# A fused attention and gated-convolution kernel on one Trainium2 core: k's last pieces ahead of the second q piece, half of w_in as two loads, and a new order on all engines

## The chip, the cores and the metric

The kernel runs on one core of a Trainium2 chip. The metric is device microseconds of one launch, as the median of several runs. A core has five engines that each work through their own instructions in order and wait for each other by semaphores: TensorE (PE; its weight loads are PEld), VectorE (DVE), ScalarE (ACT), GpSimd (POOL) and SyncE (SP). Matmuls write to PSUM, of which this kernel uses eight banks. Transfers are issued by POOL (loads that convert fp32 to bf16), by SP (loads, stores, transposes) and by ACT; they share 16 DMA engines. In the profile q0 is POOL's queue of transfers and q1 is SP's.

## What is computed

An attention without softmax, a norm over each head, then a feed-forward layer with a gate from a convolution of three taps over the sequence.

```python
def _attn_ref(q, k, v, g_norm):                  # (8, 8, 576, 64) each
    kv = np.einsum('bhsd,bhse->bhde', k, v)
    out = np.einsum('bhsd,bhde->bhse', q, kv)
    rms = np.sqrt(np.mean(out * out, axis=-1, keepdims=True) + 1e-06)
    return (out / rms * g_norm)
...
def _moe_ref(x, w_in, conv_w, w_out):            # x: (8, 576, 512), d_ff 1024
    h = np.maximum(x @ w_in, 0.0)
    ...
    for k in range(K):                           # K = 3, over the sequence
        conv_out += conv_w[k][None, None, :] * hp[:, k:k + S, :]
    gate = 1.0 / (1.0 + np.exp(-conv_out))
    return (h * gate @ w_out)
```

Inputs and output are fp32; the kernel computes in bf16 with fp32 sums.

## The kernel before

**Tiling.** There are eight batches, each with eight heads in four pairs. A pair of heads fills the 128 partitions (two times 64), with the 576 positions of the sequence as 64 partitions by 9 groups of 64 columns. A load of a whole batch of q, k or v is thus a tile of 128 x 4 x 576. Pairs are handled in two units `u` of two pairs, and the sequence in two halves `s`. Batch 0 is loaded as fp32 in pieces by SP and ACT (`HEAD` in `pre`) and cast on chip; batch 1 comes in two loads for each of q, k and v, and batches 2 to 7 in one each, from POOL.

**Steps.** For a batch: `kv` makes k transposed times v, and `kva` or `kvd` copies it out of PSUM on ACT or DVE; `qt` transposes q on TensorE and `qa` or `qd` copies it; `ot` multiplies the two; `sq`, `on` or `oq`, `nl` and `mo` do the norm and leave `x`. Then `hk`, `hs` or `hm` multiply `x` by a block `f` of 128 columns of w_in, and `rp`, `rh` or `re` apply the relu on ACT into `h`; `ta`, `aa`, `ab` (DVE), `sg` (ACT) and `mg` (DVE) make the gate and apply it; `om` multiplies 128 rows `m` of a pair of batches `p` by w_out in two halves of four blocks, `ea` (ACT) or `ed` (DVE) copies the 128 x 512 result into a buffer of the ring `row`, and `st` stores it from SP. The last rows are done in two halves of 256 columns (`oh`, `eh`, `dh`, `sh`).

**Batches 6 and 7** differ: q is transposed by a DMA (`tq`, two for each batch, one for each unit, issued on SP), k times v is done by `kz`, its result is copied to swapped partitions by two small DMAs (`kx`, SP), and `ox`, `ss`, `ln`, `sl`, `sp` and `mu` do the norm for two batches at a time.

**What sets the order.** The string `ORDER` lists every step of the kernel, with the buffer numbers behind `@`; the program is written out in that order, and a last loop ties each engine's instructions to it. A step such as `tq.6.0@1` is batch 6, unit 0, buffer 1. So each engine, and each queue of transfers, does its share of the steps in the order of the string, and a step that has to wait holds up all that stands behind it on its engine. `L` steps are loads on POOL: `Lq`, `Lk`, `Lv` with batch, first pair and number of pairs, `Li` with first block and number of blocks of w_in, `Lo` for w_out. A load writes a buffer that an earlier batch has used and so waits for that batch's last reader. `fi.n.512` is n matmuls of zeros that nothing reads.

Of the kernel before, what the change touches and what calls it, by code (L numbers as in the profile page):

```python
# [59 lines left out]
pre@0,1 af cad.q.0.0@0 cad.v.0.0@0 fi.10.512@0 qt.0.0.0@2 qd.0.0.0@0 gt.k.1.0 Li.0.4 fi.9.512@0 ct@0 Lq.1.0.2@1  # L60
Lk.1.0.2@0 Lv.1.0.2@1 Li.4.4 ps pg fi.4.512@1 cad.k.1.0@1 caa.v.1.0 caa.k.0.0 kv.0.0.1@4 kva.0.0.1@0 ot.0.0.0@6 pc
cad.v.3.0 cad.k.2.0 fi.2.512@0 cad.k.3.0 caa.q.1.0 qt.0.1.0@2 qd.0.1.0@1 sq.0.0.0@0 oq.0.0.0@4 fi.2.512@0 dg.1
caa.v.2.0 kv.0.1.1@0 fi.2.512@2 nl.0.0.0@0 kva.0.1.1 ot.0.1.0@4 sq.0.1.0@1 cad.q.0.1 qt.0.0.1@2 qa.0.0.1 fi.2.512@0
oq.0.1.0@0 nl.0.1.0@1 mo.0.0.0@0 cad.q.1.1 qt.0.1.1@6 qd.0.1.1 mo.0.1.0 ot.0.0.1@2 sq.0.0.1@2 ot.0.1.1@6 fi.1.512@0
sq.0.1.1@3 oq.0.0.1@0 nl.0.0.1@2 fi.1.512@4 fi.1.512@4 hk.0.1.0.0@4 hk.0.1.0.1 rp.1.0@0 on.0.1.1@0 nl.0.1.1@3
hk.0.2.0.0@5 hk.0.2.0.1 rp.2.0 dg.3 mo.0.0.1 dg.2 hk.0.3.0.0@4 hk.0.3.0.1 hk.0.0.0.0@2 hk.0.0.0.1 rp.0.0 hk.0.0.1.0@3
rp.3.0 hk.0.1.1.0@5 hk.0.3.1.0@0 mo.0.1.1 hk.0.3.1.1 rp.3.1 hk.0.1.1.1 rp.1.1 hk.0.0.1.1 rp.0.1 dg.0 hk.0.2.1.0@1
hk.0.2.1.1 qt.1.0.0@6 kv.1.0.1@4 rp.2.1 cv.0.2@2 sc.0.2@0 cv.0.3@0 qd.1.0.0@2 kvd.1.0.1@1 ot.1.0.1@6 sc.0.3 pl
sq.1.0.1@4 cv.0.1@4 cv.0.0@2 Lq.1.2.2 Lk.1.2.2 Lv.1.2.2 sc.0.1@1 fi.2.512@0 qt.1.1.0@0 qd.1.1.0@3 mg.0.1.1 Lo.0.8
sc.0.0 mg.0.1.0 oq.1.0.1@4 nl.1.0.1@4 mo.1.0.1@1 fi.1.512@2 hk.0.5.1.0@2 hk.0.5.0.0@3 hk.0.5.0.1 rp.5.0 hk.0.5.1.1  # L70
rp.5.1 ta.0.1.5@0 hk.0.4.1.0@0 hk.0.4.1.1 rp.4.1 hk.0.7.0.0@1 hk.0.7.0.1 kv.1.1.1@4 kvd.1.1.1 rp.7.0 ot.1.0.0@2
sq.1.0.0@5 hk.0.7.1.0@6 hk.0.7.1.1 rp.7.1 ta.0.1.7@1 ot.1.1.1@0 sq.1.1.1@6 oq.1.0.0@4 nl.1.0.0@5 mo.1.0.0 hk.0.4.0.0@6
hk.0.4.0.1 rp.4.0 hk.0.6.1.0@7 hk.0.6.1.1 rp.6.1 oq.1.1.1@4 nl.1.1.1@6 mo.1.1.1 hk.0.6.0.0@6 Lq.2.0.4@2 hk.0.6.0.1
rp.6.0 ta.0.1.4 hk.1.6.1.0@7 ta.0.1.6 hk.1.0.1.0@2 ot.1.1.0@4 sq.1.1.0@7 aa.0.1.2 hk.1.1.1.0@3 hk.1.2.1.0@6 hk.1.6.1.1
rh.1.6.1 hk.1.1.1.1 rh.1.1.1 on.1.1.0@0 nl.1.1.0@7 mo.1.1.0 hk.1.2.1.1 hk.1.5.1.0@7 hk.1.5.1.1 rh.1.5.1 rh.1.2.1
hk.1.3.1.0@3 hk.1.3.1.1 rh.1.3.1 hk.1.0.1.1 rh.1.0.1 ab.0.1.2 sg.0.1.5 sg.0.1.4 qt.2.1.0@0 qt.2.0.0@6 hk.1.5.0.0@3
hk.1.5.0.1 rh.1.5.0 qd.2.0.0@4 hk.1.0.0.0@2 hk.1.4.1.0@4 hk.1.4.1.1 hk.1.0.0.1 hk.1.1.0.0@5 hk.1.6.0.0@6 hk.1.1.0.1
hk.1.2.0.0@7 hk.1.2.0.1 rh.1.2.0 rh.1.1.0 rh.1.0.0 hk.1.6.0.1 rh.1.6.0 aa.0.1.3 qd.2.1.0@0 ab.0.1.3 sg.0.1.7 sg.0.1.6
hk.1.7.0.0@0 mg.0.1.2 hk.1.7.1.0@1 hk.1.7.1.1 rh.1.7.1 hk.1.7.0.1 rh.1.7.0 ta.1.1.1@0 ta.1.1.0 Lk.2.0.4@1 Lv.2.0.4@0
Lq.3.0.4@0 Lk.3.0.4@0 Lv.3.0.4@1 Lq.4.0.4@1 aa.1.1.0 hk.1.4.0.0@3 om.0.1.0.4@2 rh.1.4.1 hk.1.4.0.1 rh.1.4.0  # L80
om.0.2.0.4@5 kv.2.0.2@6 mg.0.1.3 om.0.1.4.4 ab.1.1.0 sg.1.1.0 sg.1.1.1 kvd.2.0.2@2 ot.2.0.1@0 sq.2.0.1@0 ed.0.1@0
st.0.1 qt.3.1.0@6 qd.3.1.0@1 Lk.4.0.4@1 Lv.4.0.4@0 Lq.5.0.4@2 om.0.2.4.4 on.2.0.1@2 qt.3.0.0@6 qd.3.0.0@2 nl.2.0.1@8
mo.2.0.1@2 om.0.3.0.4@4 ea.0.2@1 ot.2.1.1@6 ot.2.1.0@2 mg.1.1.0 om.0.3.4.4 ed.0.3@2 sq.2.1.0@1 sq.2.1.1@2 on.2.1.0@0
nl.2.1.0@9 mo.2.1.0 om.0.0.0.4@5 hk.1.3.0.0@4 on.2.1.1@0 st.0.2 nl.2.1.1@0 mo.2.1.1 om.0.0.4.4 ed.0.0@3 ot.2.0.0@2
# [54 lines left out]
def kernel(  # L139
# [46 lines left out]
    T = {}  # L186
# [638 lines left out]
```

## Time and profile before

| | us |
|---|---|
| median of 3 runs | 177.97 (177.71 to 178.49) |
| span of the profiled execution, first to last instruction | 175.6 |
| median less span | 2.4 |
| TensorE busy | 167.9 |
| VectorE busy | 149.5 |
| ScalarE busy | 148.9 |
| POOL's loads, share of the 16 DMA engines over the span | 49.2% |

The profile is of one execution, and its own time is known by its span; the 2.4 us between the span and the median stand for start and end around it. A row of the timeline gives start, duration, engine, line, operation, tiles and count, and in brackets how long the engine had been idle and what ended that. A row of the DMA view gives the transfer, the queue, the count, the size and the time from issue to landing; asked for a short window, it tells of the transfers that were issued in it. A row of a DMA queue gives packets, MB, and the time of the packets as a share of the window on 16 engines; it can pass 100% because packets overlap. The granted TensorE clock is 1.000 over the span.

### The profile page before, as it was taken

Reading aid. Unit: us, or ns where it says so; the run is one execution under the profiler, and the core shown is the slowest. Engines: PE = TensorE matmul, PEld = TensorE weight load, DVE = VectorE, ACT = ScalarE, POOL = GpSimd, SP = SyncE. Lnnn points to the kernel's source line nnn. Section 1 sums busy time; section 2 is a strip of 40 time slices with the busy share of each in tenths; the row PEclk is TensorE's granted clock in tenths of the full one; section 3 lists DMA queues with packets and bytes.
Section 4 is the critical chain, followed back from the end, with each engine's and each line's share of the span. In section 5 each row is a group of like instructions: output and inputs, shape, how many; then the busy total and the mean of one; then the engine's idle time right before and its main releaser. Section 6 shows DMA issues by size and latency. Waiting matters only on the chain.

```text
span 175.6 us, 5070 instructions
## 1 busy us (share of the span) xinstructions
PE 167.9 (96%) x2097; PEld 100.0 (57%) x2114; DVE 149.5 (85%) x290; ACT 148.9 (85%) x268; POOL 22.2 (13%) x35
## 2 busy tenths in 40 slices
PE   7979999999999999999999999999999999999992
PEld 2334766676447677644467764444877744444451
DVE  2796638899688899999999998989999999999950
ACT  2368899999978999999999998999999967676721
POOL 3094512200603013030000000000000000000000
PEclk9999999999999999999999999999999999999999
DMA  5999999999999999999999050330310003064486
GB/s 159 392 323 207 207 207 207 208 208 209 207 241 230 227 207 207 170 182 197 258 181 161 14 134 0 119 123 0 119 63 0 0 0 116 13 239 175 179 304 237
DMA packets 25911, 29.11 MB, mean 166 GB/s; under 512 B 6036, under 2 KB 20384, under 8 KB 25888
## 3 DMA queue, kind: packets, MB, share of 16 engines
q0 software_dynamic: 13296, 14.50, 49.2%
q1 hardware_dynamic: 12048, 13.11, 26.2%
q10 hardware_dynamic: 544, 1.18, 1.7%
q8 instruction: 16, 0.26, 0.6%
q14 instruction: 7, 0.06, 0.1%
HBM read 32.52 MB, written 9.44 MB: 239 GB/s over the span
## 4 chain that ended last, share of the span: by engine, by line
PE 76%; DVE 12%; ACT 5%; DMA 3%; issue 3%; ACTq 0%; DVEq 0%
PE banks L732 32%; PE banks L628 14%; PE banks L613 9%; PE banks L658 4%; DMA stg<-in_v_dram 3%; PE banks L460 3%; DVE h L722 2%; PE banks L708 2%; ACT taps L698 2%; PE banks L402 2%; PE banks L593 2%; PE banks L433 1%; PE banks L528 1%; DVE taps L681 1%; PE banks L286 1%
## 5 line engine op out<-in xcount | busy, mean ns | idle before, releaser
L732 PE MATMUL banks<-w_out_sb,h 128*128 128x512 bf16 x267 | 62.8, 379 | 1.2 <-issue 0.6
L698 ACT ACTIVATE taps<-taps,cw 128x576 bf16<-128x576 bf16 (+1 forms) x44 | 40.6, 958 | 5.7 <-DVE taps L692 5.5
L732 PEld LDWEIGHTS <-h 128*128 128x128 bf16 x280 | 26.2, 98 | 30.0 <-issue 1.1
L628 PE MATMUL banks<-x,w_in_sb 128*128 128x288 bf16 (+2 forms) x256 | 34.2, 286 | 0.0
L640 ACT ACTIVATE h<-banks 128x288 bf16<-128x288 f32 (+2 forms) x80 | 29.5, 460 | 0.3 <-PE banks L658 0.2
L628 PEld LDWEIGHTS <-w_in_sb 128*128 128x128 bf16 x256 | 24.4, 98 | 7.8 <-issue 0.8
L722 DVE TENSOR_TENSOR h<-h,taps 128x1152 bf16<-128x1152 bf16 (+1 forms) x24 | 22.8, 952 | 1.2 <-ACT taps L698 1.2
L687 DVE TENSOR_TENSOR taps<-taps 128x1152 bf16<-128x1152 bf16 (+1 forms) x22 | 21.5, 978 | 0.5
L509 ACT ACTIVATE sq<-banks 128x576 bf16<-128x576 f32 (+2 forms) x32 | 20.8, 691 | 1.1 <-PE banks L460 1.1
L692 DVE TENSOR_TENSOR taps<-taps,h 128x1152 bf16<-128x1152 bf16 (+1 forms) x22 | 21.4, 972 | 0.3
L681 DVE TENSOR_SCALAR taps<-h,cw 128x576 bf16<-128x576 bf16 (+1 forms) x44 | 18.7, 424 | 0.6 <-ACT h L665 0.5
L682 DVE TENSOR_SCALAR taps<-h,cw 128x576 bf16<-128x576 bf16 (+1 forms) x44 | 18.4, 418 | 0.0
L738 ACT ACTIVATE row<-banks 128x512 f32<-128x512 f32 x23 | 13.5, 597 | 5.7 <-PE banks L732 4.2
L658 PE MATMUL banks<-x,w_in_sb 128*128 128x288 bf16 (+2 forms) x128 | 17.7, 286 | 0.1
L613 PE MATMUL banks<-x,w_in_sb 128*128 128x288 bf16 x128 | 16.9, 286 | 0.0
L556 DVE SCALAR_TENSOR_TENSOR x<-banks,cw,rs 128x576 bf16<-128x576 f32 (+2 forms) x16 | 13.0, 816 | 3.9 <-ACT rs L545 3.6
L658 PEld LDWEIGHTS <-w_in_sb 128*128 128x128 bf16 x128 | 12.0, 98 | 4.4 <-issue 0.5
L227 ACT ACT_TABLE_LOAD x10 | 12.8, 1283 | 2.0 <-issue 1.8
L613 PEld LDWEIGHTS <-w_in_sb 128*128 128x128 bf16 x128 | 12.3, 98 | 3.7 <-issue 0.2
L443 DVE COPY qT<-banks 128x1152 bf16<-128x1152 bf16 (+2 forms) x13 | 8.8, 681 | 5.7 <-PE banks L433 5.7
L545 ACT ACTIVATE rs<-banks,eps_sb 128x576 f32<-128x576 f32 (+2 forms) x16 | 11.8, 740 | 1.1 <-PE banks L528 1.1
L599 DVE SCALAR_TENSOR_TENSOR x<-o,cw,banks 128x576 bf16<-128x576 f32 (+2 forms) x16 | 12.1, 810 | 0.7 <-PE banks L593 0.5
(89 smaller groups left out, 162.9 us busy)
## 6 DMA issues: line engine op xcount, KB each, us to landing
out_dram<-row SPq DMA_DIRECT2D x35, 256.0 KB, 2.3
q_sb<-in_q_dram POOLq DMA_DIRECT2D x6, 576.0 KB, 17.9
k_sb<-in_k_dram POOLq DMA_DIRECT2D x6, 576.0 KB, 14.5
v_sb<-in_v_dram POOLq DMA_DIRECT2D x6, 576.0 KB, 17.9
stg<-in_v_dram ACTq DMA_DIRECT2D x2, 576.0 KB, 6.2
stg<-in_k_dram SPq DMA_DIRECT2D x4, 288.0 KB, 6.9
w_in_sb<-in_moe_w_in_dram POOLq DMA_DIRECT2D x2, 512.0 KB, 9.9
w_out_sb<-in_moe_w_out_dram POOLq DMA_DIRECT2D x1, 1024.0 KB, 15.5
```

The source lines that it names most:

```text
L509: nc.scalar.activation(T["sq", b, u, s], T["o", b, u, s], AX.Square)
L613: nc.tensor.matmul(ps[:, s, :HS], w_in_sb[:, t, f * P:(f + 1) * P], T["x", b][:, t, c0:c1], start=(t == 0), stop=(t == NT - 1))
L628: nc.tensor.matmul(ps, w_in_sb[:, t, f * P:(f + 1) * P], T["x", b][:, t, c0:c1], start=(t == 0), stop=(t == NT - 1))
L640: nc.scalar.activation(h, fr, AX.Relu)
L658: nc.tensor.matmul(T[at], w_in_sb[:, t, f * P:(f + 1) * P], T["x", b][:, t, c0:c1], start=(t == 0), stop=(t == NT - 1))
L681: nc.vector.tensor_scalar_mul(tap[:, 0, f % 2, :n, 8:8 + S], h[:, f], cw[:, f:f + 1])
L682: nc.vector.tensor_scalar_mul(tap[:, 1, f % 2, :n, :S], h[:, f], cw[:, 2 * NF + f:2 * NF + f + 1])
L687: nc.vector.tensor_add(tap[:, 1, :, :n, :S], tap[:, 0, :, :n, 7:7 + S], tap[:, 1, :, :n, 1:1 + S])
L692: nc.vector.tensor_add(y, y, span(b, n)[:, 2 * j:2 * j + 2])
L698: nc.scalar.activation(y, y, AX.Sigmoid, scale=cw[:, NF + f:NF + f + 1])
L722: nc.vector.tensor_mul(h, h, tap_of(b, j)[:, 1, :, :n, :S])
L732: nc.tensor.matmul(T["om", p, m], h[:, f, m * P:(m + 1) * P], w_out_sb[:, f, :], start=(f == 0), stop=(f == NF - 1))
```

## The change

Three edits, two of which are small. In `HEAD`, SP's loads for batch 0 now bring k's third and fourth piece ahead of q's second. In `ORDER`, w_in's first four blocks come in two loads of two blocks (2 and 3, then 0 and 1) instead of one, and all other steps stand in a new order. In `kvc` and `qc` a buffer is now taken by whichever step comes first.

```diff
-pre@0,1 af cad.q.0.0@0 cad.v.0.0@0 fi.10.512@0 qt.0.0.0@2 qd.0.0.0@0 gt.k.1.0 Li.0.4 fi.9.512@0 ct@0 Lq.1.0.2@1
...
+pre@0,1 af pl ps caa.q.0.0@0 caa.v.0.0@0 fi.10.512@0 qt.0.0.0@0 qa.0.0.0@0 pn cad.v.1.0 cad.k.0.0@0 fi.7.512@2 ct@0 pg
+pc caa.k.1.0 gt.k.1.0 Li.2.2 caa.v.3.0 fi.4.512@1 kv.0.0.1@0 Li.0.2 cad.v.2.0 kva.0.0.1@0 cad.k.2.0 fi.1.512@2
...
-    HEAD = (("sync", "q.0.0 k.0.1 k.1.1 q.1.0 k.2.1 k.3.1 q.0.1 q.1.1"), ("scalar", "v.0.2 v.2.2"))
+    HEAD = (("sync", "q.0.0 k.0.1 k.1.1 k.2.1 k.3.1 q.1.0 q.0.1 q.1.1"), ("scalar", "v.0.2 v.2.2"))
...
     def kvc(eng, b, u0, n):
-        if u0 == 0:
+        if ("kvb", b) not in T:
...
     def qc(eng, b, u, s):
-        if s == 0:
+        if ("qT", b, u) not in T:
```

The work is the same but for these: 24 zero matmuls (`fi`) instead of 37, none of them behind the first `hk`; some casts and copies change between ACT and DVE; two norms change between `on` and `oq`, which sum the same numbers with full or quarter matmuls. On TensorE the steps of the later batches keep roughly their places: ahead of `kz.6.0.2`, for one, both orders have the same steps but for the zero matmuls and those norms. `kv.5.0.2` has `ot.4.1.0` and the second half of `om.0.7` ahead of it in the new order and behind it in the old.

POOL's loads behind v of batch 3 up to v of batch 6. Each row is a load of a whole batch; in the order before they are q4, k4, v4, q5, q6, k5, v5, q7, k6 and v6:

```order
L347 DMA q_sb_916<-in_q_dram 128x4x576
L347 DMA k_sb_1062<-in_k_dram 128x4x576
L347 DMA v_sb_1064<-in_v_dram 128x4x576
L347 DMA q_sb_1066<-in_q_dram 128x4x576
L347 DMA q_sb_1508<-in_q_dram 128x4x576
L347 DMA k_sb_1627<-in_k_dram 128x4x576
L347 DMA v_sb_1717<-in_v_dram 128x4x576
L347 DMA q_sb_1719<-in_q_dram 128x4x576
L347 DMA k_sb_1721<-in_k_dram 128x4x576
L347 DMA v_sb_1943<-in_v_dram 128x4x576
```

In the changed order they are k4, q5, q4, q6, k5, v4, q7, v5, k6 and v6:

```order
L347 DMA k_sb_992<-in_k_dram 128x4x576
L347 DMA q_sb_998<-in_q_dram 128x4x576
L347 DMA q_sb_1009<-in_q_dram 128x4x576
L347 DMA q_sb_1104<-in_q_dram 128x4x576
L347 DMA k_sb_1247<-in_k_dram 128x4x576
L347 DMA v_sb_1258<-in_v_dram 128x4x576
L347 DMA q_sb_1496<-in_q_dram 128x4x576
L347 DMA v_sb_1510<-in_v_dram 128x4x576
L347 DMA k_sb_1669<-in_k_dram 128x4x576
L347 DMA v_sb_1683<-in_v_dram 128x4x576
```

So v of batch 4 moves from the third place to the sixth, v of batch 5 from the seventh to the eighth, q of batch 6 from the fifth to the fourth and q of batch 7 from the eighth to the seventh; k and v of batch 6 keep theirs.

SP behind the loads of batch 0, before: stores of rows 1, 2 and 0 of the first pair of batches, tq.6.0, stores of rows 8, 3 and 4, kx.6, tq.6.1, tq.7.0:

```order
L748 DMA out_0_dram<-row_1021 128x512
L748 DMA out_0_dram<-row_1121 128x512
L748 DMA out_0_dram<-row_1163 128x512
L467 DMA_TRANSPOSE qT_1927<-q_sb_1508 128x9x128
L748 DMA out_0_dram<-row_1854 128x512
L748 DMA out_0_dram<-row_1136 128x512
L748 DMA out_0_dram<-row_1936 128x512
L489 DMA kvx_2019<-kvb_2017 64x256 x2
L467 DMA_TRANSPOSE qT_2022<-q_sb_1508 128x9x128
L467 DMA_TRANSPOSE qT_2146<-q_sb_1719 128x9x128
```

And in the changed order: the store of row 3, tq.6.0, the store of row 0, tq.7.0, the stores of rows 2 and 1, kx.6, tq.6.1:

```order
L748 DMA out_0_dram<-row_1142 128x512
L467 DMA_TRANSPOSE qT_1408<-q_sb_1104 128x9x128
L748 DMA out_0_dram<-row_1241 128x512
L467 DMA_TRANSPOSE qT_1722<-q_sb_1496 128x9x128
L748 DMA out_0_dram<-row_1120 128x512
L748 DMA out_0_dram<-row_1017 128x512
L489 DMA kvx_2023<-kvb_2013 64x256 x2
L467 DMA_TRANSPOSE qT_2033<-q_sb_1104 128x9x128
```

Here tq.6.0 stands behind one store instead of three, and tq.7.0 ahead of two stores, kx.6 and tq.6.1, behind which it stood. Each `tq` waits for its batch's q to have landed.

More of the change, by code (lines that the diff above doesn't have):

```diff
@@ L65 @@
[L65 to L84, printed above, removed]
@@ L135 @@
+st.3.0 sg.7.1.7 aa.7.1.2 om.2.6.0.4@2 ea.3.1@1 ab.7.1.2 om.2.6.4.4 st.3.1 mg.7.1.3 sg.7.1.4 om.3.7.0.4@0 ed.2.6@0
+sg.7.1.5 om.3.6.0.4@1 mg.7.1.2 om.3.4.0.4@2 om.3.6.4.4 om.3.7.4.4 ea.3.6@2 oh.3.8.0@1 ed.3.7@4 om.3.4.4.4 st.3.7
+dh.3.8.0@1 st.2.6 om.3.5.0.4@0 st.3.6 ea.3.4@5 sh.3.8.0 om.3.5.4.4 st.3.4 oh.3.8.1@1 ed.3.5@0 st.3.5 eh.3.8.1@1
+sh.3.8.1
 """
```

123 lines of the change are left out of this document (69 added, 54 removed).

## The prediction

> **What bounds the kernel now.** I read the page first: busy shares, the chain that ended last and the DMA digits.
>
> ```profile
> PE 167.9 (96%) x2097; PEld 100.0 (57%) x2114; DVE 149.5 (85%) x290; ACT 148.9 (85%) x268; POOL 22.2 (13%) x35
> ...
> DMA  5999999999999999999999050330310003064486
> ...
> PE 76%; DVE 12%; ACT 5%; DMA 3%; issue 3%; ACTq 0%; DVEq 0%
> ```
>
> TensorE sets the end: it is busy 96% of 175.6 us and holds 76% of the chain. But the DMA digits are full (9) in slices 2 to 22 of 40, about 4 to 97 us at 4.4 us a slice. So for the first half two resources are full, and the question is how far the loads run ahead of TensorE. The timeline gives the issues on POOL, the DMA view by windows the time from issue to landing, and the timeline of TensorE the first use. These are, in order, v of batch 3, q of 5, q of 6, k of 5, v of 5 and v of 6.
>
> ```profile
> 30.30 0.75 POOL L347 DMA_DIRECT2D v_sb<-in_v_dram  x1
> ...
> 45.73 0.77 POOL L347 DMA_DIRECT2D q_sb<-in_q_dram  x1
> 47.42 0.74 POOL L347 DMA_DIRECT2D q_sb<-in_q_dram  x1 [0.92 <-PE banks L433]
> 53.49 0.74 POOL L347 DMA_DIRECT2D k_sb<-in_k_dram  x1 [5.33 <-PE banks L402]
> 54.23 0.75 POOL L347 DMA_DIRECT2D v_sb<-in_v_dram  x1
> ...
> 68.69 0.75 POOL L347 DMA_DIRECT2D v_sb<-in_v_dram  x1
> ```
>
> ```profile
> v_sb<-in_v_dram POOLq DMA_DIRECT2D x1, 576.0 KB, 19.1
> ...
> q_sb<-in_q_dram POOLq DMA_DIRECT2D x1, 576.0 KB, 17.3
> ...
> q_sb<-in_q_dram POOLq DMA_DIRECT2D x1, 576.0 KB, 18.4
> ...
> k_sb<-in_k_dram POOLq DMA_DIRECT2D x1, 576.0 KB, 15.2
> v_sb<-in_v_dram POOLq DMA_DIRECT2D x1, 576.0 KB, 18.7
> ...
> v_sb<-in_v_dram POOLq DMA_DIRECT2D x1, 576.0 KB, 14.9
> ```
>
> Issue plus landing: v3 at 49.4, q5 at 63.0, q6 at 65.8, k5 at 68.7, v5 at 72.9, v6 at 83.6. From q5 to k5 lie two loads and 5.66 us, so a load of a whole batch takes **2.83 us** of the stream. It is issued 12 to 19 us before it lands: the queue is never empty, and the place in it decides. First uses, kv.5 (L402) and kz.6 (L479):
>
> ```profile
> 73.77 0.92 PE L402 MATMUL banks<-v_sb,k_sb 64*64 64x64 bf16 x72
> ...
> 80.13 0.32 PE L460 MATMUL banks<-qT,kvb 64*64 64x288 bf16 x4
> 80.38 1.04 PE L732 MATMUL banks<-w_out_sb,h 128*128 128x512 bf16 x4
> 81.35 0.67 PE L566 MATMUL banks<-sq,sel 128*32 128x288 bf16 x16
> ...
> 84.28 0.78 PE L479 MATMUL banks<-v_sb,k_sb 64*64 64x64 bf16 x72
> ```
>
> v5 is there 0.9 us before its use and v6 0.7 us before. That is all the slack: whatever puts more than a microsecond into the stream ahead of v5 or v6 stops TensorE, which works in order and has almost no idle time to give back.
>
> **What else uses the stream.** Packet counts in three windows: loads alone, with the transpose tq.6.0, and with three stores.
>
> ```profile
> q0 software_dynamic: 1750, 1.96, 120.6%
> ...
> q0 software_dynamic: 1151, 1.29, 94.1%
> q1 hardware_dynamic: 1138, 0.29, 34.9%
> ...
> q0 software_dynamic: 1423, 1.59, 92.6%
> q1 hardware_dynamic: 432, 0.79, 24.0%
> ```
>
> Alone (60 to 69.5 us) the loads move 184 packets a us. In 69.9 to 79.1 us they move 1151, which alone is worth 6.36 us at 2.83 us for 512; the other **2.84 us** of the 9.2 are the price of one transpose. In 49 to 59 us they move 1423, worth 7.87 us; the missing 2.13 us are three stores, **0.71 us** each. SP's rows give when each was issued:
>
> ```profile
> 45.67 7.92 SPq L748 DMA_DIRECT2D out_dram<-row  x3
> 65.92 2.16 SPq L467 DMA_TRANSPOSE qT<-q_sb  x1
> 79.87 5.41 SPq L748 DMA_DIRECT2D out_dram<-row  x3
> ```
>
> tq.6.0 is issued as q6 lands, yet the window to 69.5 us has no packet of q1: its service begins 4 us after issue and lasts 9 us. A check on before: v6 is the tenth load behind v3, and 49.4 + 28.3 + 2.13 + 2.84 = 82.7 against 83.6 measured, so the prices are if anything low.
>
> **The change, part by part.** *Loads.* Between v3 and v5 the old order has q4 k4 v4 q5 q6 k5, and the new one k4 q5 q4 q6 k5 v4 q7: v5 is the eighth load instead of the seventh. v6 stays tenth. *Transposes.* tq.6.0 moves to SP's second place and leaves when q6 lands; q6 is now fourth behind v3, not fifth. tq.7.0, which stood behind kx.6 and tq.6.1, moves ahead of them and of two stores, and leaves when q7 lands. So v6 now has two transposes and four stores ahead of it, where it had one and three. The first of the displaced stores waits until q7 has landed; their row buffers are wanted again by ea.0.4 only some 6 us later, so that costs nothing, and if it did, 0.6 us of ScalarE per copy would come late.
>
> *w_in's first half in two loads.* The same bytes, in rows of 512 B instead of 1024 B, twice as many packets. No row shows this size from this queue. In the transpose window a q1 packet of 256 B costs 34.9% of 16 x 9.2 us over 1138, 45 ns, and a q0 packet of 1152 B 94.1%, 120 ns; on the line between them 512 B costs 66 and 1024 B 109, so twice as many packets cost 21% more. The half now takes 2.8 us (a whole load's row, for nearly as many packets), so all later loads slip by **0.6 us**. Bounds: 0 (bytes alone count) and 2.8 (packets alone count); I take 0.6 as the row's own line.
>
> The Trainium skill, "DMA: Bandwidth & Descriptors", section "Specifications", puts the smallest transfer at line rate at 512 B; no run here shows that size, and by that rule the slip is 0 and my time 0.6 us less.
>
> *v5.* 49.4 + 0.6 + 8 x 2.83 + two stores 1.42 + tq.6.0 2.84 (issued near 62, served 66 to 75) = **76.9 us**. TensorE has ahead of kv.5 what it had before plus ot.4.1.0 and half of om.0.7; the rows at 80.13 to 81.35 price that pair at 1.2 us, so equal work is done at 73.77 + 1.2 = 75.0. It stands some 2 us longer than the old order at the same work.
>
> *v6.* 83.6 + 0.6 + one more store 0.7 + tq.7.0. That is issued as q7 lands, 49.4 + 0.6 + 19.8 + 1.4 + about 1.7 of tq.6.0 = 72.9, served from 76.9 on; by 85.4, when v6's packets end, 8.5 of its 9.2 us are over: 2.6 us. Together **87.5 us**, and kz.6, ahead of which both orders have the same real work, starts there instead of at 84.28: **+3.2 us**. The wait at kv.5 is part of it, not added.
>
> *Head and fillers.* The w_in row, its landing, the first dense matmul and the fillers:
>
> ```profile
> 8.47 0.79 POOL L361 DMA_DIRECT2D w_in_sb<-in_moe_w_in_dram  x1
> ...
> w_in_sb<-in_moe_w_in_dram POOLq DMA_DIRECT2D x1, 512.0 KB, 8.1
> ...
> 16.86 0.60 PE L658 MATMUL banks<-x,w_in_sb 128*128 128x256 bf16 x4
> ...
> 1.20 4.45 PE L286 MATMUL banks<-zero 128*128 128x512 bf16 x10 [1.20 <-DVE zero L265]
> ...
> 5.83 2.12 PE L286 MATMUL banks<-zero 128*128 128x512 bf16 x9
> ...
> 25.31 0.38 PE L286 MATMUL banks<-zero 128*128 128x512 bf16 x1
> ...
> 26.48 0.39 PE L286 MATMUL banks<-zero 128*128 128x512 bf16 x1
> ```
>
> w_in's half lands at 16.6 and dense work starts at 16.86. With columns 2 and 3 first, hk.0.2 (four matmuls of 256 columns, 0.45 us from the first row) runs before the rest lands near 17.2: a gain of 0.1 to 0.4. k's last pieces earlier let kv.0.1.1 start earlier, but the w_in gate stands behind it, so nothing of that is kept. Fillers: 13 go, three of them behind the dense start, 0.22 us each (2.12 over 9, less the tail of the last): 0.65. In all TensorE arrives 0.8 to 1.1 us earlier at kv.5, and waits that much longer: it costs and brings nothing. Were the loads in time, it would be kept.
>
> *Behind kz.6.* The same work to the end. The chain of waits shows the gaps left there:
>
> ```profile
> 85.42 0.16 issue
> ...
> 118.78 0.50 issue
> ```
>
> They and a few like them come to about 1 us; between 0 and 1 can be filled, since VectorE and ScalarE catch up during the longer stand: I take -0.3, the smaller row twice. At the end a whole-row store is now issued just ahead of the last half row instead of two half rows behind the last whole one: between 0 and one store's toll, 0.7; I take +0.2.
>
> **Sum.** +3.2 - 0.3 + 0.2 = +3.1 us, a span of 178.7 where it was 175.6. The median of the runs is 177.97, 2.4 us above the span for what lies around it, unchanged: **181.1 us**.
>
> **The rivals.** *The loads are in time (faster).* The early order keeps its 1.1 us: 176.9 us. Two points decide: slip, stores and transpose ahead of v5 cost under 3.0 us (75.0 - 49.4 - 22.6) instead of 4.9, and what is new ahead of v6 costs under 0.7 us, its slack, instead of 3.9. For it: a share of a transpose could fall into time that the loads leave unused, since the two queues together show 129% where the loads alone show 121%. Against it: 1151 load packets in the 9.2 us where 184 a us would have made 1690. Chance 0.11.
>
> *Gain and toll cancel.* tq.7.0 or the stores are served behind v6, the slip is 0: kz.6 at 84.3 to 85.2, time 177.1 to 178.8. Chance 0.09.
>
> *The clock falls.* The wait at kv.5 is 76.9 less 74.0 (75.0 less 1.0), 2.9 us. The first ten fillers take 0.445 us each, the next nine 0.236: a rested TensorE ran at about half pace for some 4.4 us, which would add 2.1 us: 183.2 us. For it: the stand is long, the longest gap in the trace of before being 1.2 us at its start. Against it: no row shows TensorE slow again after a pause, and kv.4, whose v also moves back in the queue, may take part of the wait. Chance 0.06.
>
> "TensorE: Matmul & The Clock Gate" of the Trainium skill, section "What's actually happening", halves the clock after an idle window of about 3.4 us; no run here shows such a pause in mid-kernel.
>
> *Nothing moves.* The order is a table that the program follows to the letter, so this has no chance of its own.
>
> **How the numbers follow.** Forecast 0.74 (179.3 to 182.6 us, from half a transpose less and no slip, up to a slip of 2 us). Under 0.5%, about 0.9 us, a measurement of this kernel can't be told from no change. Faster 0.11, same 0.09, slower 0.80 (forecast and clock). The range for 8 in 10 leaves out the faster case and the far upper end: 177.4 to 182.8 us.
>
> **What would show it.** Right: v5 landing at 76 to 78 and v6 at 86 to 88.5 us, L402 of kv.5 and L479 starting within 0.3 us of them, TensorE idle 2 to 3.5 us ahead of kv.5, and from L479 to the end 91 us as before. The slip: v of batch 3 landing at 50.0, not 49.4. Wrong: v6 in by 84.5, or TensorE without a gap between 65 and 90 us; and if the loss stands behind 90 us, it was the order of VectorE or ScalarE, which I have at nothing.

## The result, and the profile after

The changed kernel takes 185.95 us (median of 4 executions, 184.53 to 186.29) where the kernel before takes 177.87 us in the same series: a ratio of 1.043, 95% interval 1.0385 to 1.0469. It is slower, as forecast, but by 8.1 us and not by 3.1. The traced execution is one of 185.87 us with a span of 183.7 us; its parts below are set against the 175.6 us of before. In some executions of the new order TensorE's granted clock falls at another place as well, so where that matters a run's times stand one by one with their mean clock.

From the profile page after, busy times, clock and DMA by fortieths, and the chain that ended last:

```profile
PE 171.7 (93%) x2103; PEld 100.3 (55%) x2103; DVE 147.1 (80%) x286; ACT 152.1 (83%) x272; POOL 23.2 (13%) x36
...
PEclk9999999999999999999659999999999999999999
DMA  5999999999999999999994000303500004545254
...
PE 66%; DMA 16%; ACT 12%; issue 2%; SPq 1%; DVE 1%; POOL 0%; ACTq 0%
```

DMA has 16% of the chain where it had 3%, and the clock, which was full over the whole span before, has two slices of 6 and 5, at 87 to 96 us. The timeline of TensorE at that place (start, duration, engine, line, tiles, count, and in brackets the idle time and what ended it):

```profile
76.16 0.77 PE L402 MATMUL banks<-v_sb,k_sb 64*64 64x64 bf16 x72 [0.61 <-ACT h L640]
...
85.53 0.78 PE L479 MATMUL banks<-v_sb,k_sb 64*64 64x64 bf16 x72
86.24 0.29 PE L593 MATMUL banks<-wparts,spread 32*128 32x288 bf16 x1
88.81 0.96 PE L593 MATMUL banks<-wparts,spread 32*128 32x288 bf16 x3 [2.28 <-ACT row L738]
...
102.96 0.78 PE L479 MATMUL banks<-v_sb,k_sb 64*64 64x64 bf16 x72
```

The two rows of L479 are kz.6 and kz.7. Before, they stood at 84.28 and here:

```profile
96.55 0.79 PE L479 MATMUL banks<-v_sb,k_sb 64*64 64x64 bf16 x72
```

That cuts the span into three, and the loss of 8.1 us with it (before has one short step, ox.6.1.1 of four matmuls, ahead of kz.7 that the new order has behind it, so the second cut is sharp only to 0.2 or 0.3 us):

| | to kz.6 | kz.6 to kz.7 | kz.7 to the end |
|---|---|---|---|
| before | 84.28 | 12.27 | 79.05 |
| after | 85.53 | 17.43 | 80.74 |
| loss | 1.25 | 5.16 | 1.69 |

The forecast had 3.2, 0 and -0.1. The largest part lies where it had nothing. There TensorE waits 2.28 us for L738, the copy of an output row by ScalarE. ScalarE's row, SP's, and the DMA view of the transfers issued on SP in that time (median time from issue to landing last) say why:

```profile
88.17 0.60 ACT L738 ACTIVATE row<-banks 128x512 f32<-128x512 f32 x1 [3.76 <-DMA out_dram<-row]
```

```profile
73.43 1.92 SPq L467 DMA_TRANSPOSE qT<-q_sb  x1
75.44 1.01 SPq L748 DMA_DIRECT2D out_dram<-row  x2
```

```profile
out_dram<-row SPq DMA_DIRECT2D x2, 256.0 KB, 13.1
qT<-q_sb SPq DMA_TRANSPOSE x1, 13.2
```

The copy is ea.0.4. It writes row buffer 1, which st.0.2 still reads. That store was ready long before, but stands behind tq.7.0 in SP's queue: it is issued at 75.44 and lands 12.64 us later (the chain has it as one piece of 12.64 us), at 88.08, since its packets are served behind the transpose's: from 77 to 83 us q1 moves packets of 260 to 290 B on average, from 84 us on of 1.6 KB. The full loads' queue alone does not explain 12.64 us. In the kernel before, three stores were issued from 45.67 us on beside a loads' queue as full, with no transpose ahead of them, and landed after 6.0 to 6.5 us. ea.0.4 asks for its buffer at 84.41, 9 us after the store's issue, so a store of 6.5 us would have been in time.

ScalarE works in order and stands 3.76 us; TensorE's sp.4.1.0 needs the bank that ea.0.4 empties. And behind the pause, by windows (length, busy time of each engine with its instructions, then the granted clock, the DMA share and GB/s):

```profile
85.40:88.80 3.40, 1.13 (x74) 0.76 (x74) 0.75 (x2) 0.63 (x2) 0.00 (x0) 1.00 1.16 242
88.80:95.60 6.80, 6.64 (x29) 2.44 (x29) 3.62 (x5) 5.21 (x8) 0.00 (x0) 0.50 1.21 220
95.60:100.00 4.40, 4.40 (x37) 3.18 (x36) 4.12 (x6) 4.27 (x6) 0.00 (x0) 0.99 0.68 209
```

For 6.8 us TensorE works at half its clock.

The loads on which the forecast rested, from POOL's timeline and the DMA view, are v of batches 3, 5 and 6:

```profile
30.58 0.75 POOL L347 DMA_DIRECT2D v_sb<-in_v_dram  x1
...
64.92 0.74 POOL L347 DMA_DIRECT2D q_sb<-in_q_dram  x1 [10.09 <-PE banks L433]
65.66 0.75 POOL L347 DMA_DIRECT2D v_sb<-in_v_dram  x1
...
71.23 0.75 POOL L347 DMA_DIRECT2D v_sb<-in_v_dram  x1
```

```profile
v_sb<-in_v_dram POOLq DMA_DIRECT2D x1, 576.0 KB, 19.0
...
v_sb<-in_v_dram POOLq DMA_DIRECT2D x1, 576.0 KB, 10.4
...
v_sb<-in_v_dram POOLq DMA_DIRECT2D x1, 576.0 KB, 12.4
```

They land at 49.6, 76.1 and 83.6 us. The last was forecast at 87.5 and is no later than before. The 0.61 us that TensorE stands ahead of kv.5 (76.16) ends with v5's landing and with a relu of ScalarE that is done at 76.08; the two come together, and the profile names the relu.

Behind kz.7 there are two more waits for row buffers, one at 162 us and one in the last copy:

```profile
162.01 1.24 PE L732 MATMUL banks<-w_out_sb,h 128*128 128x512 bf16 x5 [0.64 <-ACT row L738]
...
178.45 1.04 PE L757 MATMUL banks<-w_out_sb,h 128*128 128x256 bf16 x8
...
180.11 0.38 ACT L767 ACTIVATE row<-banks 128x256 f32<-128x256 f32 x1 [2.59 <-DMA out_dram<-row]
```

From the end of the last matmul to the end of the span it is 4.24 us (183.73 less 179.49), where before had 3.38.

### The profile page after: what moved, and what is told of

It is laid out like the page before. It is cut to its first block, busy times and chain, and to the rows that moved or that the text cites. A ratio compares the mean times of both kernels' runs of the same rounds, so it can differ in the third digit from the quotient of the medians.

```text
span 183.7 us, 5066 instructions
## 1 busy us (share of the span) xinstructions
PE 171.7 (93%) x2103; PEld 100.3 (55%) x2103; DVE 147.1 (80%) x286; ACT 152.1 (83%) x272; POOL 23.2 (13%) x36
## 4 chain that ended last, share of the span: by engine, by line
PE 66%; DMA 16%; ACT 12%; issue 2%; SPq 1%; DVE 1%; POOL 0%; ACTq 0%
PE banks L732 28%; PE banks L628 13%; PE banks L613 9%; DMA out_dram<-row 8%; PE banks L658 7%; DMA w_in_sb<-in_moe_w_in_dram 4%; DMA stg<-in_k_dram 4%; ACT h L640 3%; ACT taps L698 2%; PE banks L593 2%; ACT L227 2%; ACT rs L545 1%; PE banks L460 1%; ACT taps L715 1%; PE banks L433 1%
## 5 line engine op out<-in xcount | busy, mean ns | idle before, releaser
L732 PE MATMUL banks<-w_out_sb,h 128*128 128x512 bf16 x280 | 65.2, 383 | 0.6 <-ACT row L738 0.6
L628 PE MATMUL banks<-x,w_in_sb 128*128 128x288 bf16 (+2 forms) x256 | 35.0, 291 | 0.0
L640 ACT ACTIVATE h<-banks 128x288 bf16<-128x288 f32 (+2 forms) x80 | 30.1, 471 | 1.9 <-PE banks L628 1.9
L738 ACT ACTIVATE row<-banks 128x512 f32<-128x512 f32 x24 | 14.2, 598 | 11.8 <-PE banks L732 5.7
L658 PE MATMUL banks<-x,w_in_sb 128*128 128x288 bf16 (+2 forms) x128 | 18.5, 286 | 0.4 <-DMA w_in_sb<-in_moe_w_in_dram 0.4
L743 DVE COPY row<-banks 128x512 f32<-128x512 f32 x11 | 7.5, 685 | 4.8 <-PE banks L732 2.5
## 6 DMA issues: line engine op xcount, KB each, us to landing
q_sb<-in_q_dram POOLq DMA_DIRECT2D x6, 576.0 KB, 14.7
```

The costliest lines, as they stand in the source:

```text
L628: nc.tensor.matmul(ps, w_in_sb[:, t, f * P:(f + 1) * P], T["x", b][:, t, c0:c1], start=(t == 0), stop=(t == NT - 1))
L640: nc.scalar.activation(h, fr, AX.Relu)
L658: nc.tensor.matmul(T[at], w_in_sb[:, t, f * P:(f + 1) * P], T["x", b][:, t, c0:c1], start=(t == 0), stop=(t == NT - 1))
L732: nc.tensor.matmul(T["om", p, m], h[:, f, m * P:(m + 1) * P], w_out_sb[:, f, :], start=(f == 0), stop=(f == NF - 1))
```

## The experiments

**Theory A**: the row buffer behind the transpose, and the half clock that the pause brings, make the loss. **Rival B**: the loads' stream makes it. **Rival C**: the new order of VectorE and ScalarE by itself. All edits are to `ORDER` of the changed kernel unless said otherwise; times are medians, and the ratio is to the kernel before in the same series.

**e2, other row buffers for two copies.** Nothing moves; only the buffer that ea.0.4 waits for is another.

```diff
-... om.0.6.0.4@2 ea.0.4@1 oc.5.1.1@7 ...    ... mu.4.0.1 ea.0.6@3 hs.3.5.1@4 ...
+... om.0.6.0.4@2 ea.0.4@3 oc.5.1.1@7 ...    ... mu.4.0.1 ea.0.6@1 hs.3.5.1@4 ...
```

> One edit: the copies ea.0.4 and ea.0.6 exchange row buffers (3 and 1). No load, transpose, store, matmul or copy changes its place on any engine. Theory A (a store, st.0.2, stands in SP's queue behind the transpose tq.7.0, so row buffer 1 comes free only at 88.1 us, ScalarE's copy ea.0.4 waits 3.8 us for it, TensorE 2.3 us for the bank, and its clock then falls to half for 6.8 us): TensorE's wait at 86.2 us is gone, -2.3 us, and the half clock with it, about -3 us more: 180.0 to 181.5 us. If the wait goes but the half clock has another cause: about 183.6 us. Theory B (the loss comes from the stream of loads: v of batches 5 and 6 late): 185.3 to 186.3 us, no change. Theory C (the new order of VectorE and ScalarE by itself): 185 to 186 us.

Measured 181.79 us, ratio 1.021 (1.0176 to 1.025): 4.2 us less than the changed kernel. (Three executions took 181.1 to 182.1 us, one took 186.2 at a mean clock of 0.967.) ScalarE's row in e2, in the same timeline view:

```profile
85.08 0.60 ACT L738 ACTIVATE row<-banks 128x512 f32<-128x512 f32 x1
...
89.19 0.60 ACT L738 ACTIVATE row<-banks 128x512 f32<-128x512 f32 x1 [0.40 <-DMA out_dram<-row]
```

The copy runs at 85.08 without a wait, kz.7 starts at 98.25, and the middle stretch takes 12.41 us, as before (12.27). So theory A has the whole 5.0 us of that stretch. Of these e2 keeps 4.2 in its traced execution (span 179.5): kz.6 comes 0.3 us later than in the changed kernel (the clock of this execution also falls in the head, between 14 and 20 us), and the stretch behind kz.7 takes 81.3 us where that has 80.7.

**e5, zeros in the wait.** To part the wait from the clock, TensorE gets ten matmuls on zeros that nobody reads, and the wait for the row buffer stays.

```diff
-... kz.6.0.2@0
-sp.4.1.0.4@4 ...
+... kz.6.0.2@0
+fi.10.512@4 sp.4.1.0.4@4 ...
```

> The changed kernel with ten dense matmuls on zeros (2.2 us of TensorE, results not used) put on TensorE's queue ahead of sp.4.1.0, where it waits 2.3 us for the bank; the wait for the row buffer itself stays. If the half clock of 6.8 us is the answer to TensorE's pause (theory A), it does not come: 6.83 us at half pace cost 3.4 us at most, so 182.5 to 183.5 us, with sp.4.1.0 still going on at 88.7 us. If something else brings the clock down: 185.5 to 186.5 us.

Measured 183.33 us, 182.88 in the traced execution; ratio 1.030 (1.0271 to 1.033). (Two executions at full clock took 182.8 and 182.9 us, one at 0.991 took 183.8 and one at 0.975 took 185.6; where the clock fell in these two isn't known.) TensorE's and ScalarE's timeline, and the clock by windows, of e5:

```profile
86.33 2.33 PE L286 MATMUL banks<-zero 128*128 128x512 bf16 x10
88.60 0.46 PE L593 MATMUL banks<-wparts,spread 32*128 32x288 bf16 x2
```

```profile
88.13 0.60 ACT L738 ACTIVATE row<-banks 128x512 f32<-128x512 f32 x1 [3.64 <-DMA out_dram<-row]
```

```profile
90.00:95.00 5.00, 4.93 (x38) 2.63 (x37) 4.55 (x7) 4.99 (x8) 0.00 (x0) 1.00 1.23 195
```

The copy waits as long as in the changed kernel, sp.4.1.0 goes on at 88.60 instead of 88.81, and the clock stays full. kz.6 to kz.7 takes 15.15 us (85.63 to 100.78). So of the 5.0 us between e2 and the changed kernel the wait costs 2.7 (15.15 less 12.41) and the half clock 2.3 (17.43 less 15.15).

**e1 and e11, the stores ahead of the transpose.** e1 moves the two stores in front of tq.7.0. e11 instead moves tq.7.0 back behind kx.6 and tq.6.1, where it stood before, and has the two edits of e6 besides.

```diff
-tq.7.0@0 sq.4.0.0@0 ...  oc.4.1.0@2 st.0.2 ed.0.7@4 Lk.7.0.4@1 st.0.1 ...
+st.0.2 st.0.1 tq.7.0@0 sq.4.0.0@0 ...  oc.4.1.0@2 ed.0.7@4 Lk.7.0.4@1 ...
```

> Only SP's queue changes: the stores st.0.2 and st.0.1 leave ahead of the transpose tq.7.0. Theory A: row buffer 1 is free by 72 us, no wait at 86 us and no half clock, about -5.3 us, and the two stores' toll of 0.7 us each comes ahead of v of batch 5, whose matmuls already wait 0.6 us for it, so up to +1.4 us: 180.3 to 182.2 us. Theory B: v of batch 5 is later by up to 1.4 us and nothing is won: 186 to 187.4 us.

> The changed kernel with the transpose tq.7.0 back behind kx.6 and tq.6.1, and the two edits behind 110 us of e6; row buffers as in the changed kernel. Theory A: the two stores no longer stand behind a waiting transpose, leave at 65 us, and ea.0.4 finds its buffer; their toll of 1.4 us falls ahead of v of batch 5, whose wait grows to 2 us as in e1_stores_first, perhaps with some half clock: 179.5 to 181.5 us. If the transpose's own traffic, not the stores behind it, made the loss: 178.0 to 178.8 us. If neither: about 183 us (the changed kernel less 2.8).

Measured 182.96 us (ratio 1.031, 1.0267 to 1.0348) and 181.10 us (1.020, 1.0185 to 1.0215). In neither does ea.0.4 wait, and kz.6 to kz.7 takes 11.9 us in both. But their toll ahead of v of batch 5 is there too. TensorE in e1, and the clock behind that wait:

```profile
77.54 0.77 PE L402 MATMUL banks<-v_sb,k_sb 64*64 64x64 bf16 x72 [2.08 <-DMA v_sb<-in_v_dram]
```

```profile
75.40:78.80 3.40, 1.28 (x80) 0.93 (x79) 0.78 (x3) 1.76 (x5) 0.17 (x1) 1.00 1.21 207
78.80:82.20 3.40, 3.39 (x15) 1.02 (x15) 2.79 (x5) 2.80 (x6) 1.31 (x2) 0.51 1.20 200
```

A second place, another cause of the pause, and the same answer: 3.4 us at half clock behind a wait of 2.08 us. In e11 TensorE waits 2.08 us at the same place and the clock stays full:

```profile
75.00:80.00 5.00, 2.92 (x89) 1.55 (x88) 2.60 (x6) 3.56 (x8) 0.27 (x1) 1.00 1.21 206
80.00:85.00 5.00, 5.00 (x51) 2.02 (x49) 5.00 (x7) 4.95 (x9) 1.21 (x2) 1.00 1.21 207
```

So a pause of 2 us may bring the clock down and need not. In both kernels the wait moved from the middle to kv.5, and kz.6 comes at 88.25 and 87.76 us. (e11's mean clock is 0.99 in all four executions; in the traced one it falls in the head, between 14 and 20 us.)

**e3 and e7, v of batch 5 ahead of q of batch 7.** e3 is the changed kernel with this edit, e7 is e6 with it.

```diff
-Lq.7.0.4@1 hs.2.7.1@6 sg.1.1.4 hs.3.0.0@7 qd.4.1.0@2 Lv.5.0.4@1 ...
+Lv.5.0.4@1 hs.2.7.1@6 sg.1.1.4 hs.3.0.0@7 qd.4.1.0@2 Lq.7.0.4@1 ...
```

> Only POOL's queue changes: v of batch 5 is loaded ahead of q of batch 7. Theory B (loads' order): v5 lands 2.8 us earlier, the wait of 0.6 us ahead of its matmuls goes, 185.0 to 185.5 us. Theory A: q7 lands 2.8 us later, the transpose tq.7.0 and the store st.0.2 behind it leave later, row buffer 1 comes free later, and the wait in the middle grows by 1 to 2.8 us: 186.3 to 188.5 us.

> e6 with v of batch 5 loaded ahead of q of batch 7. Theory B's part: the wait of 0.5 us at kv.5 goes, -0.5 to -0.8 us from e6, 178.9 to 179.6 us. Theory A's rule: tq.7.0 and with it st.0.2 leave 1 to 2.8 us later, and the copy ea.0.6, which now has row buffer 1, waits: 180 to 183 us.

e3 took 184.5, 190.0, 190.2 and 190.2 us, e7 183.3, 186.2, 186.7 and 186.7; all four of e7 are slower than e6's 179.0. The traced execution of e7 (186.2 us) shows the rule of theory A at its clearest. ScalarE, then TensorE:

```profile
93.11 0.60 ACT L738 ACTIVATE row<-banks 128x512 f32<-128x512 f32 x1 [4.12 <-DMA out_dram<-row]
```

```profile
93.76 1.03 PE L593 MATMUL banks<-wparts,spread 32*128 32x288 bf16 x4 [3.83 <-ACT row L738]
```

v5 comes in time, but q7 lands 6 us later, tq.7.0 waits for it on SP, the two stores wait behind tq.7.0, and the copy that wants row buffer 1 (now ea.0.6) waits 4.1 us. In e7 an earlier load made the kernel slower because of what stands behind the later one. e3 is no such evidence. Its traced execution is its one of 184.47 us; there the store, issued at 79.88, lands after 8.42 us, and ea.0.4 waits 1.55 us, less than in the changed kernel and not more as theory A had it. What makes the other three 5.7 us longer stays open.

**e4, row buffers of the last copies.**

```diff
-... oh.3.8.1@1 ed.3.5@0 st.3.5 eh.3.8.1@1
+... oh.3.8.1@1 ed.3.5@3 st.3.5 eh.3.8.1@4
```

> The last copies ed.3.5 and eh.3.8.1 get row buffers that are free (3 and 4 in place of 0 and 1). All theories of the middle: no change there. The tail's 4.24 us from the last matmul to the end, where before had 3.38, shrinks by 0.5 to 0.8 us if it is the wait for a row buffer that lengthens it: 185.0 to 185.5 us; if the last store's own transfer sets the end: no change.

Measured 186.05 us (ratio 1.049, 1.0435 to 1.0546), no gain. The last copy starts 0.5 us earlier, but its store takes 2.8 us instead of 2.2 and lands no sooner, at 182.8 where the changed kernel has 182.7. The last transfers set the end, not the wait for the buffer.

**e6, the two places behind 110 us.** On top of e2, st.1.5 moves up in SP's queue, and the last whole row goes ahead of both half rows.

```diff
-... ea.1.3@3 ... st.1.3 ... st.2.5 ... st.1.5 ...
+... ea.1.3@3 ... st.1.3 st.1.5 ... st.2.5 ...
...
-... ea.3.6@2 oh.3.8.0@1 ed.3.7@4 om.3.4.4.4 st.3.7 dh.3.8.0@1 ... sh.3.8.0 om.3.5.4.4 st.3.4 oh.3.8.1@1 ed.3.5@0 st.3.5 eh.3.8.1@1 sh.3.8.1
+... ea.3.6@2 ed.3.7@4 om.3.4.4.4 st.3.7 ... om.3.5.4.4 st.3.4 oh.3.8.0@1 ed.3.5@3 st.3.5 eh.3.8.0@1 sh.3.8.0 oh.3.8.1@3 dh.3.8.1@4 sh.3.8.1
```

> The edit of e2_row_buffer and two more behind 110 us: the store st.1.5 stands right behind st.1.3 in SP's queue, so that ea.2.2 finds row buffer 0 free (ScalarE waited 2.8 us for it, TensorE 1.1 us), and the program ends with the last whole row and then both half rows, as before had it. If these two waits are what is left behind 98 us: -1.1 and -0.8 us from the 181.8 of e2_row_buffer, 179.5 to 180.3 us. If they are covered by other work: 181.0 to 181.8 us.

Measured 179.01 us, ratio 1.009 (1.0054 to 1.0125). kz.7 to the end takes 79.2 us (97.66 to 176.89) where the changed kernel has 80.7, e2 81.3 and before 79.05, so nearly the whole loss behind kz.7 is these two places: 2.0 of the 2.6 us between the spans of e2 and e6. The rest lies between kz.6 and kz.7 (11.91 us against 12.41), where the two kernels do not differ; in e2's traced execution ea.0.6 still waits 0.40 us for a store there, in e6's it does not.

What is left, 1.3 us of the span, lies ahead of kz.6, at 85.75 in e6 against 84.28. More than a third of that is there before TensorE waits for v of batch 5. At its first row of L708 the changed kernel is 0.2 us ahead of the one before (21.78 against 21.98). Then it stands 0.30 and 0.16 us at 28 and 29 us, where before had no wait. It is through with all that stands ahead of kv.5 at 75.55 (e6 at 75.62), where the prediction's price for the same work in the old order gives 75.0. (Apart from the zeros, the work ahead of kv.5 differs beyond that pair only in three norms, not two, that change between `on` and `oq`.)

**e9, e12 and e14, work ahead of kv.5.** e9 puts kv.5 behind om.0.5.0 in e6, e12 does so in e11, and e14 (on e13) puts om.0.5's first half ahead of kv.5 and its second behind.

```diff
-... ot.4.1.0@4 kv.5.0.2@0 ... ot.4.1.1@6 ... om.0.5.0.4@2 kvd.5.0.2@1 ...
+... ot.4.1.0@4 ... ot.4.1.1@6 ... om.0.5.0.4@2 kv.5.0.2@0 kvd.5.0.2@1 ...
```

> e6 with kv.5 (72 matmuls that need v of batch 5) put four dense matmuls later in TensorE's order, behind om.0.5.0. Theory B's remainder: what is left of the loss in e6 (about 1.2 us over before) is the wait of 0.8 to 0.9 us for v of batch 5 at 75.4 us; it goes, 178.0 to 178.4 us. If it only moves on to the next piece that needs a late load or copy: 178.8 to 179.2 us.

> e11 with kv.5 later as in e9. Theory B's wait for v5 shrinks by 0.9 us and TensorE's pause stays under 1.5 us, so no half clock: 178.4 to 179.6 us. If half the clock comes back all the same: 180 to 181 us.

> e13 with the first half of om.0.5 ahead of kv.5 and the second half between kv.5 and ot.5.0.0, so that both the wait for v of batch 5 (0.9 us) and the copy of its result (0.8 us in e9) have dense work beside them. If the remainder is this wait: 177.4 to 177.9 us. If the time is set by the loads further on (v of batch 6 and the transposes): 178.0 to 178.6 us.

Measured 178.81 us (1.0067, 1.0052 to 1.0082), 180.53 us (1.0154, 1.0122 to 1.0186) and 180.29 us (1.0154, 1.014 to 1.0168): little or nothing won, and 0.7 us lost in e14 against e13. (Of e12, one execution at a clock of 0.999 took 179.4 us and three at 0.99 took 180.4 to 180.8; in the traced one, at 0.99, the clock falls in the head, between 14 and 20 us, and not at kv.5.) In e9 kv.5 no longer waits and the wait stands at the next piece that needs its result:

```profile
76.83 0.78 PE L402 MATMUL banks<-v_sb,k_sb 64*64 64x64 bf16 x72
78.22 0.44 PE L460 MATMUL banks<-qT,kvb 64*64 64x288 bf16 x8 [0.61 <-DVE kvb L414]
```

**e8, e17 and e18, is it ScalarE?** e8 has v5 first and the stores first, with e6's edits behind 110 us. e17 and e18 put three copies that the change gave to ScalarE back on VectorE, in e8 and in e6.

```diff
-... ab.1.1.2 ea.0.1@0 ...   ... kva.2.0.2@0 ...   ... kva.3.0.2@0 ...
+... ab.1.1.2 ed.0.1@0 ...   ... kvd.2.0.2@0 ...   ... kvd.3.0.2@0 ...
```

> v of batch 5 ahead of q of batch 7, the stores st.0.2 and st.0.1 ahead of tq.7.0, and the two edits behind 110 us of e6; row buffers as in the changed kernel. The stores' toll of 1.4 us and the load's 2.8 us about cancel at v5, so neither kv.5 nor ea.0.4 should wait: theory A 178.6 to 179.6 us. If the wait for v5 stays at 2 us as in e1_stores_first: 180.5 to 181.5 us.

> e8 with three of the copies that the change moved from VectorE to ScalarE put back on VectorE (ea.0.1 and the two copies of kv in batches 2 and 3): 1.4 us less work on ScalarE ahead of 65 us, where VectorE stands. Theory C for the remainder (ScalarE works without a pause from 53 to 76 us, so TensorE's 0.75 us at 75.0 us in e8 is a wait for ScalarE's queue): that wait goes, 177.9 to 178.4 us where e8 had 178.9 in its undisturbed executions. If the remainder is not ScalarE's: 178.7 to 179.2 us.

> The same three copies on VectorE in e6. There v of batch 5 lands at 76.24 us and ScalarE's copy ahead of it ends at 76.15 us, so if two limits end together, taking one away brings little: 178.7 to 179.0 us against e6's 179.0. If ScalarE alone held TensorE at 75 us: 178.1 to 178.5 us.

e8 took 178.9 and 179.2 us at full clock (182.1 and 182.5 at 0.987 and 0.988): no better than e6, though v5 is 4.5 us earlier, because TensorE stands 0.75 us one step ahead of kv.5 without it; the profile names nothing that ended this. e17 took 179.2, 179.6 and 180.2 us (one more execution ran at about half clock from the start, 278 us, and is left aside), e18 180.78 us (ratio 1.0185, 1.0143 to 1.0226). Both are slower, not faster: in e18 TensorE now stands 0.88 us at 46.4 us for the copy of the row, which waits its turn among VectorE's work. Where the last microsecond goes was not settled; what is shown is that taking the wait for v5 away does not bring it back.

**e10, e15: w_in's first half.** e10 puts it in one load again in e6; e15 is the kernel before with the one load made two, and nothing else.

```diff
-... Li.0.4 ...
+... Li.2.2 Li.0.2 ...
```

> e6 with w_in's first half in one load again. If twice as many packets of half the size hold up the loads behind them by the 0.6 us of the forecast: v of batch 3 lands 0.6 us earlier and the time is 178.3 to 178.6 us. If the slip is the 0.16 us that the changed kernel's landing shows: 178.8 to 179.2 us. If the split brings TensorE's dense work forward and that is kept: 179.2 to 179.5 us.

> The kernel before with one edit: w_in's first half in two loads. If the split costs the 0.66 us that its removal brought in e10: 178.1 to 178.5 us, ratio 1.003 to 1.005. If it costs the 0.16 us by which v of batch 3 was later in the changed kernel: 177.6 to 177.9 us, ratio 1.000 to 1.0015.

e10 took 178.2 to 178.3 us in three executions of full clock (179.7 at 0.99 and 181.4 at 0.979 in two more), 0.7 us less than e6. e15 took 177.74 us, ratio 1.0006 (0.9996 to 1.0015, 11 executions): the split costs nothing there. The pair e13 and e16 below differs by the split alone and by 0.03 us. So the 0.7 us of e10 is no price of the split that holds elsewhere.

**e13 and e16, zeros back in the head.** e13 is e10, and e16 is e6, with eight of the zero matmuls put back at four places.

```diff
-... ot.0.1.0@2 ... ot.0.0.1@4 ... ot.0.1.1@0 ... oq.0.0.1@6 ...
+... fi.3.512@2 ot.0.1.0@2 ... fi.2.512@4 ot.0.0.1@4 ... fi.2.512@0 ot.0.1.1@0 ... fi.1.512@6 oq.0.0.1@6 ...
```

> e10 (w_in's half in one load) with eight dense matmuls on zeros put back into the head, ahead of ot.0.1.0, ot.0.0.1, ot.0.1.1 and oq.0.0.1, where TensorE stands 0.4 to 0.7 us each time at 12 to 15.5 us. Theory D (the changed order took 13 zero matmuls out, the head has so many short stands that the clock sometimes falls to half at 16 to 21 us, which costs 1.2 to 3 us in such an execution): no execution with a clock under 0.995, all within 178.0 to 178.7 us. If the head's half clock does not come from the missing work: one in three executions at 179.5 to 181.5 us as in e10.

> e6 (two loads) with the eight zero matmuls of e13 in the head. Theory D: no execution with a clock under 0.995, 178.8 to 179.1 us, so that the split's price against e13 is again 0.6 to 0.7 us. If the split's price was chance: within 0.2 us of e13.

Measured 179.57 us (1.0111, 1.0097 to 1.0125) and 179.54 us (1.0109, 1.0095 to 1.0123). The mean clock was 0.996 or more in all 12 executions of e13, e14 and e16, and in all 44 of the kernel before; without these zeros it was 0.99 or less in 5 of 17 in e6, e8, e9 and e10, and in 10 of 12 in e11, e12 and e18. Not every such fall is known to lie in the head: the traces of e2, e3, e7, e10, e11 and e12 have one there. The clock half of the expectation came true, the time did not: the zeros cost 0.5 to 1.2 us against an execution of full clock. The windows of e10's traced execution, which has a fall, then the first of them in before and in e6:

```profile
11.50:14.90 3.40, 2.20 (x103) 1.66 (x102) 2.96 (x10) 3.21 (x6) 2.22 (x4) 1.00 1.24 224
14.90:21.70 6.80, 6.50 (x33) 3.50 (x34) 3.09 (x6) 4.67 (x9) 4.48 (x6) 0.50 1.21 204
```

```profile
11.50:14.90 3.40, 3.23 (x101) 1.59 (x98) 2.93 (x9) 2.64 (x6) 3.07 (x4) 1.00 1.24 226
```

```profile
11.50:14.90 3.40, 2.32 (x106) 1.68 (x102) 2.93 (x10) 3.05 (x6) 2.47 (x4) 1.00 1.40 216
```

TensorE is busy 2.20 of 3.40 us there instead of 3.23. But it is as little busy in e6 (2.32) and in the changed kernel (2.19), and in these two traced executions no fall follows in the head. So missing work of this size allows a fall and does not bring one each time. None of the kernels in the new order beats the one before; the nearest is e10 with 178.33 us.

## Why the prediction was wrong, point by point

- **The step that failed** is the one on the displaced stores: that their row buffers "are wanted again by ea.0.4 only some 6 us later, so that costs nothing, and if it did, 0.6 us of ScalarE per copy would come late." It took the store for done within those 6 us, and the stores of before, with no transpose ahead of them, did land in 6.0 to 6.5. It had priced tq.7.0 itself at 13 us from issue to the end of its service, and did not ask how long a store takes that is issued behind it: 12.64 us, where ea.0.4 left it 9. The wait is 3.76 us of ScalarE and 2.28 of TensorE (2.7 us of the stretch by e2 and e5), and it was bounded at 0.6.
- **The half clock** was a rival with a chance of 0.06, put at kv.5 and priced at 2.1 us. It came at sp.4.1.0, cost 2.3 us (e5), and needed a pause of only 2.3 us. At kv.5, where the rival had it, the wait was 0.6 us. In e1, where that wait is 2.08 us, the clock does fall there (in e11, after as long a wait, it does not). So the rival's mechanism was right, and its place hung on the step above. That its price was near is in part luck: it had 4.4 us at half pace, and 6.8 were measured.
- **v5** was forecast for 76.9 and TensorE ready for it at 74.0. It landed at 76.1 and TensorE was ready at 75.55, so the idle time was 0.6 us instead of 2.9.
- **v6** was the term of +3.2 us, from 83.6 + 0.6 + 0.7 + 2.6 = 87.5. It landed at 83.6, and kz.6 came 1.25 us late. The transposes were mis-sized: 2.84 us of the stream each was taken from a window in which the loads' queue was full. The working took the loads' queue for never empty, and in the changed kernel it nearly ran out twice. POOL stands 10.09 us ahead of q7 for its buffer, only v of batch 4 is left in the loads' queue when tq.6.0 is served, and tq.6.0, issued at 61.79, lands after 6.9 us, where in e7 with one load more in the queue it takes 14.7. Of tq.7.0, q1 moved some 660 packets from 77 to 81 us beside loads at 118 to 170 packets a us; another 480 went from 81 to 83 us, when POOL's queue was down to 11 to 15 a us. It landed at 86.6. And the two displaced stores were served behind v6, so that it had two stores ahead of it and not four.
- **The split of w_in**, 0.6 us: v of batch 3 landed at 49.6, 0.2 later than before, and e15 finds 0.1 us (interval -0.1 to 0.3). The lower bound, 0, by which bytes alone count, was the right end. By the rule of the Trainium skill, "DMA: Bandwidth & Descriptors", "Specifications", that 512 B is enough for line rate, it is also 0, and e15 agrees.
- **Behind kz.6**, -0.3 + 0.2 = -0.1 us, was +1.7 besides the middle: st.1.5 late in SP's queue, another case of the failed step, and a tail of +0.86 where 0.2 was taken and 0.7 was the bound.
- **Head and fillers** were to bring TensorE to kv.5 0.8 to 1.1 us early, to be lost in the wait there. It came 0.55 us late (75.55 against 75.0 for equal work). It was 0.2 early at 22 us, after standing 0.42 us at 16.94 for the second of w_in's two loads; the waits at 28 and 29 us are 0.46 of what it lost behind that, the rest is open. What the forecast did not have is that fillers keep the head's clock up (e13 and e16 against e6 and e10).
- **The test that was named held in part**: "if the loss stands behind 90 us, it was the order of VectorE or ScalarE, which I have at nothing". Of 8.1 us, 6.9 stand behind kz.6, and most of it behind a copy of ScalarE, though what was late was SP's queue.

## What to carry to other kernels

A store in a queue is part of the life of the buffer it reads: when a transfer that must wait for its input is moved ahead of a store, take the time from the store's readiness to its landing behind that transfer, and look up who writes its buffer next. A wait on TensorE can have two prices, the wait and the clock behind it, and zeros in the wait part the two in one run. An earlier load is only a gain if what stands behind the load that is put off can wait.

## What the hardware showed

- TensorE's clock fell in pieces of 3.4 us: one piece in e1 (78.8 to 82.2 us), two in the changed kernel (88.8 to 95.6) and in e10's head (14.9 to 21.7). The Trainium skill, "TensorE: Matmul & The Clock Gate", section "What's actually happening", tells of a free-running window of 3413 ns, and the traces agree with its length. They differ on what fills it: no window had to be idle. The longest pause ahead of a fall in the middle was 2.28 us in the changed kernel and 2.08 in e1, so that every stretch of 3.4 us there had work in it (1.13 and 1.28 us in the two that are shown). In the head 2.20 us of short matmuls came ahead of a fall in e10, but 2.19 in the changed kernel and 2.32 in e6 did not. That like stretches sometimes lower the clock and sometimes not, as does the same wait of 2.08 us in e1 and in e11, would fit a window that runs free of the kernel; no run here shows where the windows lie.
- A store of 256 KB took 2.4 us from issue to landing in the median of the whole program. Beside a full loads' queue it took 6.0 to 6.5 us (before), and behind a transpose in its own queue, with the loads' queue full beside that transpose, 12.64 us (changed kernel, loads until 81 us) and 13.5 in the median of three (e8). Behind a transpose with little left in the loads' queue it took 7.3 and 7.1 us in the median of three (e1, e11).
- The same transpose tq.6.0 took 6.9 us in the changed kernel, with one load left in the loads' queue beside it. With two loads there it took 14.7 us in e7 and 11.2 in e3, and in the kernel before 14.3.
